# One-hots of a routing step on GpSimd instead of VectorE, and the keys of two heads in alternate partitions of the value buffers

## The chip, the cores and the metric

One core of one Trainium2 chip runs the whole kernel. The metric is the device time of an execution in microseconds; of the kernel before there are three runs with a median of 599.23 us. The engines are called TensorE (PE), VectorE (DVE), ScalarE (ACT), GpSimd (POOL) and SyncE (SP), the short names being those of the profile. SP issues most of the transfers.

## The reference

Windowed attention, and behind it a two-level mixture of experts on its output. Cut to what matters:

```python
batch, n_heads, seq, head_dim = (8, 8, 576, 64)
mask_plain = (rel >= 0) & (rel < 32)                      # heads 0 to 3
mask_dil = (rel >= 0) & (rel < 128) & (rel % 4 == 0)      # heads 4 to 7
scores = np.where(masks, scale * (q @ k.T), -1e9)
attn = exp(scores - max) ; attn = attn / (sum + 1e-09)
x = (attn @ v).transpose(0, 2, 1, 3).reshape(4608, 512)

g_logits = x @ w_group            # 4 groups: g_idx = argmax, g_w = its softmax
e_logits = x[g] @ w_expert[g]     # 4 experts a group: e_idx, e_w
for each of the 16 experts:
    h = np.maximum(xg[mask_e] @ w1[g, e], 0.0)            # 512 -> 1024
    ye = h @ w2[g, e]                                     # 1024 -> 512
    out[tok_idx] = (g_w * e_w)[:, None] * ye
```

## The kernel before

Attention runs in 36 steps n = 0 to 35, each for 64 positions of two batches and all heads, twelve groups of three steps. The loop over s from 0 to 38 works on several steps at once: `scores(s)`, `av(s - 2)`, `transpose_p(s - 1)`, `softexp(s)`, `transpose_x(s - 3)` and `normalise(s - 2)`. For one step TensorE makes the masked scores (L250, L267); VectorE takes the maximum mx (L277) and subtracts it into d (L279); ScalarE exponentiates d; TensorE transposes that (L292) into pt; then 32 matmuls (L304, `av`) multiply it with the values and with a column of ones for the sum; VectorE turns the sum into den (L353, L355) and writes the normalised x (L360). TensorE transposes x (L381) for the routing, and SP stores x to a buffer xd in device memory, three steps at a time.

The values of a group lie in `vt`, three buffers of 128 partitions, [2, 3, 8, 65] values in each: the first index is the head's half r, the second one j the step within the group. Keys of half r stand in partitions 64r to 64r + 63, in plane r; the other plane of these partitions is zero, so that one matmul over all 128 partitions serves both halves. A second copy `vs`, shifted by half a block, is made by GpSimd (`shift_v`, L128 to L138). The zeros are written at the start by ScalarE (vt[0]) and by VectorE's memsets (L916), one or two at the end of each of the first steps. Keys (`load_k`, buffers kb) already lie in alternate partitions; the third buffers of the queries and of the values are part of `wa`, which later holds weights.

Routing is done in four routes, one for each pair of batches (1152 tokens, TPB = 9 tiles of 128). `route(bp)` is a generator: matmuls of x with the router's weights, the arg-max as one-hots, the rank of each token among those of its expert by matmuls with a triangle (rk_ps), and so a slot number for each token (slots). The slot is cut into a high and a low part (sli, hl). Two sets of one-hots follow: `mv`, 9 x 64 wide, which is the token's number where the high part fits, and `ohl`, 9 x 128 wide, which is 1 where the low part fits. Nine matmuls (tb_ps, L498) add their products up into the table that says which token stands in which slot. The gains (s5, es, sg, gt) and the table's update follow.

The order of TensorE, VectorE, ScalarE and SP is that in which the code is written; only GpSimd's is set by a scheduler. A route's pieces are put between the attention's instructions by `slot()`: it stands twice in `scores`, twice in `normalise` and once in the loop, and each call runs the route up to its next `yield 0`. A `yield 2` sets `gate`, and the route goes on only after TensorE's queue has passed the next `av`. `pick(r)` chooses the two experts that start early (`early`), while attention still runs: their rows are gathered (xe), transposed (L672) and cast (xs, L673, L674). Weights come in by SP, ScalarE makes the upper half of their precision (L615) and VectorE the lower half (L612). After the last step the fourth route runs among the first matmuls of the early experts (L697).

```python
def slot():
    for _ in range(0 if gate else fine[0]):
        if run(routes) == 2:
            gate.append(1)
            break
```

Of the kernel before, what the change touches and what calls it, by code (L numbers as in the profile page):

```python
# [8 lines left out]
F32 = mybir.dt.float32  # L9
# [8 lines left out]
P = 128  # L18
# [5 lines left out]
NE = 16  # L24
# [31 lines left out]
def moe_attention_kernel(ctx, tc, q, k, k0, v, cmask, wgate, wpack, out):  # L56
# [47 lines left out]
    off = lambda t, r: t[64 * r : 64 * r + 64, 1 - r].rearrange("p j s c -> p (j s c)")  # L104
# [16 lines left out]
    def load_v(g, cuts=(0, 3)):  # L121
        for j0, j1 in zip(cuts, cuts[1:]):
            for r in range(2):
                at = slice(64 * r, 64 * r + 64)
                nc.sync.dma_start(vt[three(g)][at, r, j0:j1], v[g, at, j0:j1])

    def shift_v(g, j0=0, j1=3):
        to, own, last = vs[g % 2], vt[three(g)], vt[three(g - 1)]  # L128
        for r in range(2):
            odd, even = slice(64 * r, 64 * r + 32), slice(64 * r + 32, 64 * r + 64)  # L130
            nc.gpsimd.tensor_scalar(to[even, r, j0:j1], own[even, r, j0:j1], 1.0, 1.0, ALU.mult, ALU.mult)
            for j in range(j0, j1):
                if j > 0:
                    nc.gpsimd.tensor_scalar(to[odd, r, j], own[odd, r, j - 1], 1.0, 1.0, ALU.mult, ALU.mult)
                elif g % 3 == 0:
                    nc.gpsimd.memset(to[odd, r, 0], 0.0)
                else:
                    nc.gpsimd.tensor_scalar(to[odd, r, 0], last[odd, r, 2], 1.0, 1.0, ALU.mult, ALU.mult)  # L138
# [8 lines left out]
    for t in kb:  # L147
        nc.vector.memset(t[:, 0], 0.0)
        nc.scalar.activation(t[:, 1], id32[:, 0:1].broadcast_to([P, KW]), AF.Copy, scale=0.0)
    for r in range(2):  # L150
        z = id32[64 * r : 64 * r + 64, 0:1].broadcast_to([64, VW // 2])
        nc.scalar.activation(off(vt[0], r), z, AF.Copy, scale=0.0)
    zeros = [off(t, r) for t in (vs[0], vt[1], vs[1], vt[2]) for r in range(2)]
# [7 lines left out]
    load_q(1)  # L161
    load_v(1)
    load_q(2)
# [39 lines left out]
    mine1 = cp.tile([P, TPB], F16, name="mine1")  # L203
# [42 lines left out]
    def scores(n):  # L246
# [28 lines left out]
        d = ap.tile([P, 8, 64], F32, name="d", bufs=2)  # L275
# [3 lines left out]
        nc.vector.tensor_tensor(d, s, mx.unsqueeze(2).broadcast_to([P, 8, 64]), ALU.subtract)  # L279
# [8 lines left out]
    def transpose_p(n):  # L288
        p = st.pop(n)
        t = psT.tile([P, 4, P], F32, name="t", tag="t")  # L290
        for c in range(4):
            nc.tensor.transpose(t[:, c, :], p[:, 2 * c : 2 * c + 2, :].rearrange("p a b -> p (a b)"), id32)  # L292
# [100 lines left out]
    def route(bp):  # L393
# [52 lines left out]
        for t in range(TPB):  # L446
# [29 lines left out]
        nc.vector.tensor_tensor(  # L476
            mv,
            high.rearrange("p e k -> p (e k)").unsqueeze(1).broadcast_to([P, TPB, NE * NK4]),
            hl[:, 1].unsqueeze(2).broadcast_to([P, TPB, NE * NK4]),
            ALU.is_equal,  # L480
        )
        yield 0
        nc.vector.tensor_tensor(mv, mv, mine1.unsqueeze(2).broadcast_to([P, TPB, NE * NK4]), ALU.mult)
        yield 0
        ohl = T("ohl", [TPB, P], F16)
        for t0 in range(0, TPB, 3):
            nc.vector.tensor_tensor(
                ohl[:, t0 : t0 + 3],
                low16.unsqueeze(1).broadcast_to([P, 3, P]),
                hl[:, 0, t0 : t0 + 3].unsqueeze(2).broadcast_to([P, 3, P]),  # L490
                ALU.is_equal,
            )
            if t0 < TPB - 3:
                yield 0
# [8 lines left out]
        yield 0  # L503
# [6 lines left out]
        yield 0  # L510
# [10 lines left out]
        yield 0  # L521
# [9 lines left out]
    def pick(r):  # L531
# [3 lines left out]
        yield 0  # L535
# [12 lines left out]
        yield 0  # L548
# [344 lines left out]
    for s in range(NT + 3):  # L893
# [60 lines left out]
    while routes:  # L954
        run(routes)
    run(eq, 100)
# [227 lines left out]
```

## Time and profile before

| what | value |
| --- | --- |
| median of 3 runs | 599.23 us (597.15 to 601.65) |
| profiled execution | 596.25 us, span 594.5 us |
| mean granted clock of TensorE | 0.981 |
| busy share of the span | PE 92%, DVE 66%, ACT 54%, POOL 34% |

The profiled execution is one of its own, 1.75 us longer than its span. Shares are means over the whole span: TensorE is busy nearly all of the last two thirds and has its gaps in the first. Of the other engines it matters when they are done, more than how much they work.

### The profile page before, as it was taken

Reading aid. Unit: us, or ns where it says so; the run is one execution under the profiler, and the core shown is the slowest. Engines: PE = TensorE matmul, PEld = TensorE weight load, DVE = VectorE, ACT = ScalarE, POOL = GpSimd, SP = SyncE. Lnnn points to the kernel's source line nnn. Section 1 sums busy time; section 2 is a strip of 40 time slices with the busy share of each in tenths; the row PEclk is TensorE's granted clock in tenths of the full one; section 3 lists DMA queues with packets and bytes.
Section 4 is the critical chain, followed back from the end, with each engine's and each line's share of the span. In section 5 each row is a group of like instructions: output and inputs, shape, how many; then the busy total and the mean of one; then the engine's idle time right before and its main releaser. Section 6 shows DMA issues by size and latency. Waiting matters only on the chain. (4 is left out here: it accounts for less than half of the span.)

```text
span 594.5 us, 16716 instructions
## 1 busy us (share of the span) xinstructions
PE 544.9 (92%) x6644; PEld 392.4 (66%) x6644; DVE 394.5 (66%) x872; ACT 319.9 (54%) x568; POOL 203.1 (34%) x248
## 2 busy tenths in 40 slices
PE   4787999888697699999999999999999999999995
PEld 3666777677475457756666665756757657777883
DVE  6874595896786852556486859767476587567750
ACT  6344454553664423646364646546676566657641
POOL 6864656552401040422124152222622502202211
PEclk9999999998989799999999999999999999999999
DMA  8998988889757433495969779697897998998750
GB/s 258 304 266 227 264 245 234 250 227 229 254 142 254 132 108 139 115 299 163 244 188 289 201 240 211 218 306 203 273 244 226 300 272 237 294 298 258 246 152 29
DMA packets 83011, 134.33 MB, mean 226 GB/s; under 512 B 43532, under 2 KB 53174, under 8 KB 82930
## 3 DMA queue, kind: packets, MB, share of 16 engines
q1 hardware_dynamic: 76002, 113.65, 67.3%
q0 software_dynamic: 6784, 19.51, 10.3%
q8 instruction: 54, 0.88, 0.7%
q14 instruction: 27, 0.22, 0.2%
q10 hardware_dynamic: 144, 0.07, 0.0%
HBM read 106.16 MB, written 19.29 MB: 211 GB/s over the span
## 5 line engine op out<-in xcount | busy, mean ns | idle before, releaser
L705 DVE SCALAR_TENSOR_TENSOR hl<-a,hh 128x256 f16<-128x256 f32 (+13 forms) x144 | 60.9, 424 | 82.2 <-ACT hh L704 82.1
L761 POOL DMA_INDIRECT out<-yr,sent x31 | 34.0, 1096 | 216.4 <-ACT yr L760 204.8
L697 PE MATMUL a<-xs,wb1h 128*128 128x256 f16 (+7 forms) x576 | 99.7, 279 | 6.7 <-DVE xs L674 3.5
L697 PE MATMUL a<-xs,wa 128*128 128x304 f16 (+7 forms) x864 | 96.7, 272 | 1.8 <-DVE hl L705 1.8
L612 DVE SCALAR_TENSOR_TENSOR wa<-w,wa 128x1024 f16<-128x1024 f32 x64 | 77.8, 1224 | 28.4 <-ACT wa L615 28.4
L697 PEld LDWEIGHTS <-wa 128*128 128x128 f16 x864 | 79.3, 98 | 18.1 <-issue 2.1
L704 ACT ACTIVATE hh<-a 128x256 f16<-128x256 f32 (+13 forms) x144 | 55.8, 387 | 63.9 <-PE a L697 63.0
L790 PEld LDWEIGHTS <-hh 128*128 128x128 f16 x480 | 46.9, 98 | 54.6 <-issue 1.2
L615 ACT ACTIVATE wa<-w 128x1024 f16<-128x1024 f32 x64 | 67.2, 1054 | 22.7 <-DMA w<-wpack 21.6
L697 PE MATMUL a<-xs,wb1l 128*128 128x256 f16 (+7 forms) x288 | 79.4, 279 | 0.0
L790 PE MATMUL y<-wa,hh 128*128 128x512 f16 x240 | 73.9, 379 | 0.0
L697 PEld LDWEIGHTS <-wb1h 128*128 128x128 f16 x576 | 55.7, 99 | 16.3 <-issue 3.6
L304 PE MATMUL o<-vs,pt 128*32 128x130 f32 x576 | 43.1, 286 | 18.0 <-DVE x L360 14.6
L293 ACT COPY pt<-t 128x512 f32<-128x512 f32 x36 | 21.1, 586 | 67.9 <-PE t L292 67.9
L640 POOL DMA_INDIRECT xr<-xd,sent x41 | 41.9, 1022 | 39.9 <-DVE key L569 16.4
L612 DVE SCALAR_TENSOR_TENSOR wb2l<-w,wb2h 128x1024 f16<-128x1024 f32 x32 | 38.9, 1223 | 22.7 <-ACT wb2h L615 22.6
L304 PEld LDWEIGHTS o<-vs,pt 128*32 128x32 f32 x576 | 34.0, 114 | 23.1 <-issue 13.8
L760 ACT ACTIVATE yr<-y,cs 128x512 f32<-128x512 f32 (+3 forms) x31 | 21.3, 686 | 49.7 <-PE y L790 34.3
L790 PE MATMUL y<-wb2h,hl 128*128 128x512 f16 x120 | 45.5, 379 | 0.3 <-DVE hl L705 0.3
L790 PE MATMUL y<-wb2h,hh 128*128 128x512 f16 x120 | 45.6, 380 | 0.0
L790 PE MATMUL y<-wb2l,hh 128*128 128x512 f16 x120 | 45.5, 379 | 0.0
L790 PE MATMUL y<-wa,hl 128*128 128x512 f16 x120 | 45.5, 379 | 0.0
(199 smaller groups left out, 1072.8 us busy)
## 6 DMA issues: line engine op xcount, KB each, us to landing
w<-wpack SPq DMA_DIRECT2D x128, 512.0 KB, 5.1
kb<-k SPq DMA_DIRECT2D x24, 384.0 KB, 4.9
qb<-q SPq DMA_DIRECT2D x22, 256.0 KB, 4.1
xd<-x SPq DMA_DIRECT2D x24, 192.0 KB, 4.1
vt<-v SPq DMA_DIRECT2D x16, 260.0 KB, 5.9
vt<-v SPq DMA_DIRECT2D x16, 130.0 KB, 5.1
wa<-v SPq DMA_DIRECT2D x6, 260.0 KB, 8.9
xd<-x SPq DMA_DIRECT2D x32, 48.0 KB, 4.5
```

What stands on the lines that cost most here:

```text
L293: nc.scalar.copy(pt[n % NPT], t)
L304: nc.tensor.matmul(o[32 * j : 32 * j + 32, c // 2, at : at + 130], pt[n % NPT][:, c, 32 * j : 32 * j + 32], t[:, :, jl, bb * 4 + c, :], st ...
L612: nc.vector.scalar_tensor_tensor(l, w32, SW, h, ALU.mult, ALU.subtract)
L615: nc.scalar.mul(parts(i)[0], w32s[i], SW)
L640: nc.gpsimd.indirect_dma_start(out=xr[0:n], out_offset=None, in_=xd[0:known, :], in_offset=bass.IndirectOffsetOnAxis(ap=ent[0:n, t : t + 1 ...
L697: nc.tensor.matmul(a[:, 0:cap], ww[:, c * FF + f * P : c * FF + f * P + P], xx[:, c, 0:cap], start=(i == 0), stop=(i == len(mm) - 1),)
L704: nc.scalar.activation(hh[:, f, 0:cap], a[:, 0:cap], AF.Relu)
L705: nc.vector.scalar_tensor_tensor(hl[:, f, 0:cap], a[:, 0:cap], 0.0, hh[:, f, 0:cap], ALU.max, ALU.subtract)
L760: nc.scalar.activation(yr[0:n, :], yp[0:n, :], AF.Copy, scale=cs[0:n, t : t + 1])
L761: ins = nc.gpsimd.indirect_dma_start(out=out, out_offset=bass.IndirectOffsetOnAxis(ap=ent[0:n, t : t + 1], axis=0), in_=yr[0:n, :], in_off ...
L790: nc.tensor.matmul(yp, h[:, f, t * P : t * P + n], ww[:, f * DM : f * DM + DM], start=(i == 0), stop=(i == len(mm) - 1),)
```

## The change

Five things are changed.

1. `load_v` puts the value rows of half r into partitions r, r + 2, ..., so that the keys of both halves alternate. The exponentiated scores get the same order: d becomes [128, 4, 64, 2], written by the subtract with a stride of two, and the transposes read it without a stride. `shift_v` then works on 64 partitions and both planes at once: four instructions a group instead of eight, each with twice the columns, zeros among them.
2. The zeros: vt[0] is zeroed whole, one plane by VectorE and one by GpSimd, vt[1] by one instruction of ScalarE, vt[2] by one memset of VectorE in step 0. The copies vs need none now. The eight memsets in the first steps are gone.
3. At the start the queries of group 2 are loaded ahead of the values of group 1.
4. In routes 0 to 2 all one-hots are made by GpSimd, an `ohl` and an `mv` for each of the nine tiles, 18 instructions with per-partition operands (hl, mine1, now 32 bits) in place of VectorE's five. Route 3 has its `ohl` on GpSimd and its `mv` on VectorE as before. A `yield 2` more stands ahead of the table's matmuls in routes 0 to 2, and several `yield 0` are gone, so that two instructions run in one slot.
5. An expert whose turn has come when the routes are drained is started there.

```diff
     def load_v(g, cuts=(0, 3)):
         for j0, j1 in zip(cuts, cuts[1:]):
             for r in range(2):
-                at = slice(64 * r, 64 * r + 64)
-                nc.sync.dma_start(vt[three(g)][at, r, j0:j1], v[g, at, j0:j1])
+                nc.sync.dma_start(vt[three(g)][r:P:2, r, j0:j1], v[g, 64 * r : 64 * r + 64, j0:j1])
...
-        for r in range(2):
-            odd, even = slice(64 * r, 64 * r + 32), slice(64 * r + 32, 64 * r + 64)
-            nc.gpsimd.tensor_scalar(to[even, r, j0:j1], own[even, r, j0:j1], 1.0, 1.0, ALU.mult, ALU.mult)
+        odd, even = slice(0, 64), slice(64, P)
+        nc.gpsimd.tensor_scalar(to[even, :, j0:j1], own[even, :, j0:j1], 1.0, 1.0, ALU.mult, ALU.mult)
+        for j in range(j0, j1):
+            if j > 0:
+                nc.gpsimd.tensor_scalar(to[odd, :, j], own[odd, :, j - 1], 1.0, 1.0, ALU.mult, ALU.mult)
...
+        if i == 0:
+            nc.vector.memset(vt[0][:, 0], 0.0)
+            nc.gpsimd.memset(vt[0][:, 1], 0.0)
...
-    zeros = [off(t, r) for t in (vs[0], vt[1], vs[1], vt[2]) for r in range(2)]
+    flat = lambda t: t.rearrange("p w j s c -> p (w j s c)")
+    nc.scalar.activation(flat(vt[1]), id32[:, 0:1].broadcast_to([P, VW]), AF.Copy, scale=0.0)
...
     load_q(1)
+    load_q(2)
     load_v(1)
-    load_q(2)
...
-        nc.vector.tensor_tensor(d, s, mx.unsqueeze(2).broadcast_to([P, 8, 64]), ALU.subtract)
+        nc.vector.tensor_tensor(
+            d.rearrange("p c k w -> p c w k"),
+            s.rearrange("p (c w) k -> p c w k", w=2),
+            mx.rearrange("p (c w) -> p c w", w=2).unsqueeze(3).broadcast_to([P, 4, 2, 64]),
+            ALU.subtract,
+        )
...
-        hl = T("hl", [2, TPB], F16)
+        hl = T("hl", [2, TPB])
         nc.vector.tensor_copy(hl[:, 1], sli[:, 1])
-        yield 0
         nc.vector.scalar_tensor_tensor(hl[:, 0], hl[:, 1], -float(P), slots[:, mine], ALU.mult, ALU.add)
         yield 0
         mv = T("mv", [TPB, NE * NK4], F16)
...
         ohl = T("ohl", [TPB, P], F16)
-        for t0 in range(0, TPB, 3):
+        if bp == NBP - 1:
             nc.vector.tensor_tensor(
-                ohl[:, t0 : t0 + 3],
-                low16.unsqueeze(1).broadcast_to([P, 3, P]),
-                hl[:, 0, t0 : t0 + 3].unsqueeze(2).broadcast_to([P, 3, P]),
+                mv,
+                high.rearrange("p e k -> p (e k)").unsqueeze(1).broadcast_to([P, TPB, NE * NK4]),
+                hl[:, 1].unsqueeze(2).broadcast_to([P, TPB, NE * NK4]),
                 ALU.is_equal,
             )
-            if t0 < TPB - 3:
-                yield 0
+            nc.vector.tensor_tensor(mv, mv, mine1.unsqueeze(2).broadcast_to([P, TPB, NE * NK4]), ALU.mult)
+        for t in range(TPB):
+            nc.gpsimd.tensor_scalar(ohl[:, t], low16, hl[:, 0, t : t + 1], None, ALU.is_equal)
+            if bp < NBP - 1:
+                nc.gpsimd.tensor_scalar(
+                    mv[:, t],
+                    high.rearrange("p e k -> p (e k)"),
+                    hl[:, 1, t : t + 1],
+                    mine1[:, t : t + 1],
+                    ALU.is_equal,
+                    ALU.mult,
+                )
+        if bp < NBP - 1:
+            yield 2
         yield 2
...
-        for _ in range(2 if s == 0 else 1):
-            if zeros:
-                nc.vector.memset(zeros.pop(0), 0.0)
+        if s == 0:
+            nc.vector.memset(flat(vt[2]), 0.0)
...
+    for r in picked:
+        if r not in ev:
+            expert(r)
```

Lines of the changed kernel differ by a few from those of the kernel before (tb_ps is L502 there, x L363, d L277). VectorE's order around the one-hots of route 2, from the cast of hl on, in the kernel before (wa is a weight half, den and x belong to step 32, mx and d to step 34):

```order
L471 CAST hl<-sli 128x9
L473 SCALAR_TENSOR_TENSOR hl<-hl,slots 128x9
L279 TENSOR_TENSOR d<-s,mx 128x512
L476 TENSOR_TENSOR mv<-high,hl 128x576
L483 TENSOR_TENSOR mv<-mv,mine_209 128x576
L353 TENSOR_SCALAR den<-o 128x8
L487 TENSOR_TENSOR ohl<-low_177,hl 128x384 x2
L355 RECIPROCAL den<-den 128x8
L487 TENSOR_TENSOR ohl<-low_177,hl 128x384
L360 TENSOR_TENSOR x<-o,den 128x512
L612 SCALAR_TENSOR_TENSOR wa<-w_2558,wa 128x1024
```

and in the changed one:

```order
L473 CAST hl<-sli 128x9
L474 SCALAR_TENSOR_TENSOR hl<-hl,slots 128x9
L611 SCALAR_TENSOR_TENSOR wa<-w_2521,wa 128x1024
L275 TENSOR_REDUCE mx<-s 128x8
L277 TENSOR_TENSOR d<-s,mx 128x4x2x64
L356 TENSOR_SCALAR den<-o 128x8
L358 RECIPROCAL den<-den 128x8
L363 TENSOR_TENSOR x<-o,den 128x512
L611 SCALAR_TENSOR_TENSOR wa<-w_2523,wa 128x1024
L275 TENSOR_REDUCE mx<-s 128x8
```

The five one-hot instructions are gone from between d and x, and the weight half stands behind hl, ahead of mx.

GpSimd's order around the one-hots of route 0 in the changed kernel (vs from vt are value shifts of group 6, vs from wa those of group 5; in the kernel before the rows of shifts follow each other there):

```order
L128 TENSOR_SCALAR vs_109<-wa 64x2x520
L131 TENSOR_SCALAR vs_109<-wa 64x2x520
L128 TENSOR_SCALAR vs_108<-vt_106 64x2x1040
L131 TENSOR_SCALAR vs_108<-vt_106 64x2x520
L487 TENSOR_SCALAR ohl<-low_178,hl 128x128
L489 TENSOR_SCALAR mv<-high,hl,mine_210 128x64
```

Sixteen more of ohl and mv in turn follow; behind these come the shifts of the last third of the group:

```order
L489 TENSOR_SCALAR mv<-high,hl,mine_210 128x64
L131 TENSOR_SCALAR vs_108<-vt_106 64x2x520
L128 TENSOR_SCALAR vs_108<-vt_106 64x2x520
L135 TENSOR_SCALAR vs_109<-vt_106 64x2x520
L128 TENSOR_SCALAR vs_109<-vt_107 64x2x1040
```

TensorE's order at the end of a step of route 2 in the kernel before (t and tx are transposes, L304 is the attention's second matmul):

```order
L304 MATMUL o<-vs_109,pt_113 32x130
L304 MATMUL o<-vt_106,pt_113 32x130
L292 MATMUL t<-id_76,d 128x128 x4
L381 MATMUL tx<-id_76,x 128x128 x4
L498 LDWEIGHTS ohl
L498 MATMUL tb_ps<-mv,ohl 128x64
```

and at the same step in the changed one:

```order
L307 MATMUL o<-vs_109,pt_113 32x130
L307 MATMUL o<-vt_106,pt_113 32x130
L295 MATMUL t<-id_76,d 128x128 x4
L384 MATMUL tx<-id_76,x 128x128 x4
L671 MATMUL pt<-id_76,xe_220 128x128 x4
L307 MATMUL o<-vs_109,pt_112 32x130
```

The nine matmuls of the table have moved behind the next step's transposes; those of routes 0 and 1 stand where they stood.

## Rows read from the trace of the kernel before

**Rows 1.** The profile page, part 2: TensorE's busy tenths in 40 slices
```profile
PE   4787999888697699999999999999999999999995
```

**Rows 2.** Waits of TensorE, 0 to 226 us: us in total, times, longest
```profile
PE o L304 <- DVE x L360: 14.6, 11, 3.9
PE s L267 <- DMA kb<-k: 6.7, 3, 3.7
...
PE a L697 <- DVE xs L674: 3.5, 1, 3.5
```

**Rows 3.** Timeline, 158 to 170 us: start, us, engine, line, operation
```profile
158.72 0.16 DVE L471 CAST hl<-sli 128x9 f16<-128x9 int32 x1
...
159.59 0.75 DVE L476 TENSOR_TENSOR mv<-high,hl 128x576 f16<-128x576 f16 x1
...
160.38 0.76 DVE L483 TENSOR_TENSOR mv<-mv,mine 128x576 f16<-128x576 f16 x1
...
161.13 1.01 DVE L487 TENSOR_TENSOR ohl<-low,hl 128x384 f16<-128x384 f16 x2
...
162.60 0.68 DVE L360 TENSOR_TENSOR x<-o,den 128x512 f32<-128x512 f32 x1
...
163.43 0.61 PE L304 MATMUL o<-vs,pt 128*32 128x130 f32 x2 [3.93 <-DVE x L360]
...
168.81 0.43 PE L304 MATMUL o<-vs,pt 128*32 128x130 f32 x1
```

**Rows 4.** Windows: length, busy us by engine (count), granted clock, DMA share, GB/s
```profile
28.00:36.00 8.00, 6.06 (x126) 4.71 (x126) 6.05 (x11) 2.94 (x8) 7.22 (x11) 1.00 0.99 289
160.00:162.00 2.00, 0.00 (x0) 0.00 (x0) 1.97 (x5) 2.00 (x5) 0.00 (x0) 1.00 0.82 246
164.00:166.00 2.00, 2.00 (x33) 1.61 (x26) 1.97 (x5) 0.00 (x0) 0.00 (x0) 0.50 0.66 149
```

**Rows 5.** Timeline of SP's queue, 48 to 58 us
```profile
53.55 0.52 SPq L113 DMA_DIRECT2D kb<-k  x1
```

**Rows 6.** Groups of VectorE by form: busy us, mean ns, idle before
```profile
L916 DVE MEMSET vs<- 64x1560 f32 x4 | 5.4, 1358 | 1.3 <-issue 1.3
```

**Rows 7.** Waits of TensorE, 16 to 54 us
```profile
PE o L304 <- DVE x L360: 2.9, 3, 1.5
```

**Rows 8.** Waits of TensorE, 80 to 90 us
```profile
PE o L304 <- DVE x L360: 0.8, 1, 0.8
PE o L304 <- DVE hl L473: 0.4, 1, 0.4
```

**Rows 9.** Waits of TensorE, 116 to 126 us
```profile
PE o L304 <- DVE x L360: 1.7, 2, 1.1
```

**Rows 10.** Groups of GpSimd (POOL) by form
```profile
L134 POOL TENSOR_SCALAR vs<-vt 32x520 f32<-32x520 f32 x36 | 23.0, 641 | 4.3 <-PE o L304 1.9
L131 POOL TENSOR_SCALAR vs<-vt 32x1040 f32<-32x1040 f32 x18 | 19.0, 1054 | 12.2 <-DMA vt<-v 10.4 <-PE o L304 0.8
...
masks.py:199 POOL TENSOR_SCALAR_AFFINE_SELECT id<-id 128x128 f32<-128x128 f32 x1 | 0.3, 291 | 0.1
```

**Rows 11.** Timeline, 79 to 88 us
```profile
79.67 0.92 DVE L471 CAST hl<-sli 128x9 f16<-128x9 int32 x1
...
80.64 1.21 POOL L134 TENSOR_SCALAR vs<-vt 32x520 f32<-32x520 f32 x2
...
87.58 0.43 PE L498 MATMUL tb_ps<-mv,ohl 128*128 128x64 f16 x9
```

**Rows 12.** Groups of ScalarE by form
```profile
L388 ACT COPY xT<-tx 128x256 f32<-128x256 f32 x24 | 15.5, 647 | 0.0
...
L383 ACT COPY xT<-tx 128x256 f32<-128x256 f32 x36 | 13.2, 366 | 8.0 <-PE lt_ps L406 6.7 <-PE tx L381 1.2
```

**Rows 13.** The profile page, part 6: DMA issues, KB each, us to landing
```profile
kb<-k SPq DMA_DIRECT2D x24, 384.0 KB, 4.9
...
vt<-v SPq DMA_DIRECT2D x16, 260.0 KB, 5.9
```

More of the change, by code (lines that the diff above doesn't have):

```diff
@@ L123, in load_v @@
             for r in range(2):
-                at = slice(64 * r, 64 * r + 64)
-                nc.sync.dma_start(vt[three(g)][at, r, j0:j1], v[g, at, j0:j1])
+                nc.sync.dma_start(vt[three(g)][r:P:2, r, j0:j1], v[g, 64 * r : 64 * r + 64, j0:j1])
     def shift_v(g, j0=0, j1=3):
         to, own, last = vs[g % 2], vt[three(g)], vt[three(g - 1)]
-        for r in range(2):
-            odd, even = slice(64 * r, 64 * r + 32), slice(64 * r + 32, 64 * r + 64)
-            nc.gpsimd.tensor_scalar(to[even, r, j0:j1], own[even, r, j0:j1], 1.0, 1.0, ALU.mult, ALU.mult)
[L132 to L138, printed above, removed]
+        odd, even = slice(0, 64), slice(64, P)
[3 more added lines that the diff above has]
+                nc.gpsimd.tensor_scalar(to[odd, :, j], own[odd, :, j - 1], 1.0, 1.0, ALU.mult, ALU.mult)
+            elif g % 3 == 0:
+                nc.gpsimd.memset(to[odd, :, 0], 0.0)
+            else:
+                nc.gpsimd.tensor_scalar(to[odd, :, 0], last[odd, :, 2], 1.0, 1.0, ALU.mult, ALU.mult)
     first = ExitStack()
@@ L146, in moe_attention_kernel @@
     nc.gpsimd.memset(k0t[:, 1, 0 : 8 * 96], 0.0)
-    for t in kb:
+    for i, t in enumerate(kb):
         nc.vector.memset(t[:, 0], 0.0)
         nc.scalar.activation(t[:, 1], id32[:, 0:1].broadcast_to([P, KW]), AF.Copy, scale=0.0)
-    for r in range(2):
-        z = id32[64 * r : 64 * r + 64, 0:1].broadcast_to([64, VW // 2])
-        nc.scalar.activation(off(vt[0], r), z, AF.Copy, scale=0.0)
-    zeros = [off(t, r) for t in (vs[0], vt[1], vs[1], vt[2]) for r in range(2)]
+        if i == 0:
[3 more added lines that the diff above has]
+    nc.scalar.activation(flat(vt[1]), id32[:, 0:1].broadcast_to([P, VW]), AF.Copy, scale=0.0)
     for w in range(2):
@@ L202, in moe_attention_kernel @@
     )
-    mine1 = cp.tile([P, TPB], F16, name="mine1")
+    mine1 = cp.tile([P, TPB], F32, name="mine1")
     nc.gpsimd.iota(
@@ L274, in scores @@
         s = s.rearrange("p c w k -> p (c w) k")
-        d = ap.tile([P, 8, 64], F32, name="d", bufs=2)
+        d = ap.tile([P, 4, 64, 2], F32, name="d", bufs=2)
         mx = ap.tile([P, 8], F32, name="mx")
@@ L291, in transpose_p @@
         for c in range(4):
-            nc.tensor.transpose(t[:, c, :], p[:, 2 * c : 2 * c + 2, :].rearrange("p a b -> p (a b)"), id32)
+            nc.tensor.transpose(t[:, c, :], p[:, c].rearrange("p k w -> p (k w)"), id32)
         nc.scalar.copy(pt[n % NPT], t)
@@ L502, in route @@
         nc.vector.tensor_scalar_add(s5, s5, 1e-9)
-        yield 0
         es = T("es", [TPB, 4])
@@ L509, in route @@
         nc.vector.tensor_reduce(sg, es, axis=AX.X, op=ALU.add)
-        yield 0
         nc.vector.tensor_tensor(sg, sg, s5v[:, :, 0], ALU.mult)
@@ L534, in pick @@
         nc.vector.tensor_tensor(cnt, base[AFTER[r]], base[0], ALU.subtract)
-        yield 0
         key = T("key", [NE])
@@ L547, in pick @@
         nc.vector.tensor_tensor(kk, top[:, r], iota[:, 0:NE], ALU.mult)
-        yield 0
         nc.vector.tensor_reduce(km, kk, axis=AX.X, op=ALU.add)
```

12 lines of the change are left out of this document (removed).

## The prediction

> **What bounds the kernel now.** I read the page first, then the waits of TensorE, then the stretches where it waits. From the fifteenth slice, about 208 us, to the end the slices of TensorE show nines [rows 1]: there the experts run, nothing waits, and what the front gains or loses passes to the end one for one. All of the change lies in front of that. There TensorE's largest wait is on VectorE: 14.6 us in 11 waits stand between the attention's second matmul (L304) and the normalised output x (L360); the keys' transfers (kb) cost 6.7 us in three waits, and the first experts' input xs 3.5 us in one [rows 2]. TensorE's queue is in program order, so such a wait delays all behind it. A step needs only some 2.1 us of VectorE for mx, d and x (x 0.68 [rows 3], the others alike), less than TensorE's part of it, so VectorE is late only where something is put between: zeroing at the start, one-hots in each of four routes.
>
> Two other limits must be kept in view. In 28 to 36 us the DMA share is 0.99 [rows 4]. And SP's own issue row shows a transfer of keys sent only at 53.55 [rows 5], after a burst of x stores; TensorE then waits for it, the 3.7 us of [rows 2].
>
> **The change part by part.** The sum is made against the profiled execution, 596.25 us; the median of the runs shown, 599.23, is 3.0 us above it, which I add at the end.
>
> **Zeroing at the start.** Eight 64x1560 memsets of 1.36 us each, of which [rows 6] group four, leave steps 0 to 7. One of 3120 columns (by the same rate 2.7 us) comes to step 0, and one of 1.36 us stands ahead of that, both while TensorE still waits for its first loads. Its waits on x between 16 and 54 us are 2.9 us in three [rows 7], so 2.9 is the most that can be won; the least is nothing, because the transfers run full to 36 us [rows 4] and the next wait on keys can grow by what was won. I take 2.0: the stores that stand on SP ahead of that late transfer also come earlier when x does.
>
> **One-hots of routes 0 and 1.** VectorE loses five instructions a route: two for mv (0.75 and 0.76) and three for ohl at about 0.50 [rows 3]. The waits of TensorE that they make are 0.8 and 0.4 us in route 0 [rows 8] and 1.7 in route 1 [rows 9], 2.9 in all. GpSimd takes 18 instructions instead. Its price p for one is not in the trace, so I bound it. A 128x128 select took 0.29 us; a copy of 520 columns took 0.64 and one of 1040 columns 1.05 [rows 10], a line with a foot of 0.23 and 0.0008 per column, so 0.33 for 128 columns and 0.28 for 64. The lower end is 0.25, the upper the 520-column price, 0.64. I take 0.27 on average, as the select has the very shape, and the half-width mv is cheaper still: 18 x 0.27 = 4.9 us a route. Is that covered? In route 0 the value shifts end at 80.64 + 1.21 = 81.85 [rows 11], with hl ready by then, so the one-hots end near 86.8. TensorE reached the table's matmuls (tb_ps) at 87.58 [rows 11] after 1.2 us of waits that now are gone: 86.4. It would wait 0.4 us, in general 18p - 4.5. In route 1 the same working (there GpSimd is free a little sooner) leaves 18p - 6.0. The value shifts become fewer and longer (64 partitions with two heads' columns; by the line 6.2 us a group for 7.0), and VectorE is slowed beside them: a 9-column cast took 0.92 us beside a shift [rows 11] against 0.16 with GpSimd idle [rows 3]. I charge 0.5 us for that. Net: 2.9 - 0.4 - 0.5 = 2.0 won.
>
> No row shows an instruction of GpSimd with a per-partition operand. [...]
>
> **Route 2.** This is the largest term. Ahead of the x that ends at 163.28 VectorE runs mv at 159.59 and 160.38 and ohl from 161.13 on, three in two pieces [rows 3]. TensorE waits 3.93 us for that x, until 163.43 [rows 3], and its granted clock is then 0.50 in 164 to 166, the lower of its two levels, after 1.00 in the idle 160 to 162 [rows 4]. Without these 3.0 us x can start when its den is there, near 159.8, and end at 160.5: the wait falls to about 1.1. Waits up to 1.5 us [rows 7] cost no clock in their stretch, so I expect no fall. Before, the next L304 block came at 168.81 [rows 3], with the one at 163.43 run at half the clock. Now the block is over before 162, and the next is set by VectorE: weight cast, mx, d, x (1.2 + 3 x 0.68 from 160.5, with den between) and the transposes bring it to about 164.6. That is 4.2 us earlier, less up to 0.7 if the route's normaliser instructions (s5, es, sg) fall into the next step's path, plus as much if they are hidden. The order shows the table's nine matmuls one step later, behind the next step's transposes; GpSimd has from 159.6 to about 166.9, so 18p - 7.3 is the wait there, none at my price. I take 4.0; 2.4 if the clock falls all the same, 4.8 at best.
>
> **Route 3.** Only the three ohl (3 x 0.50) leave VectorE, ahead of the casts for xs that TensorE waits on for 3.5 us [rows 2]; GpSimd's nine take 9 x 0.29 = 2.6 us beside that wait. I take 1.4, with 0 to 1.5 as ends.
>
> **At no cost, and what covers them.** The subtract that now writes d with a stride of two: bounded by ScalarE's copies of 256 columns, 0.37 us and 0.65 us by the place they write [rows 12], so nothing or 0.3 to 0.6 us more a step; outside the routes VectorE's slack covers it, which idles for a quarter of 28 to 36 us with memsets still in it [rows 4]. Two instructions to a slot, and the gain copy with its DMA a few places earlier on ScalarE and SP: the same instructions, their places in queues that wait there for other things. The value loads into alternate partitions: 260 KB land in 5.9 us now where 384 KB of keys, already laid so, land in 4.9 [rows 13]; at nothing here, a rival below.
>
> Sum: 2.0 + 2.0 + 4.0 + 1.4 = 9.4, less 0.8 that I let the keys' wait at step 21 swallow, which stands behind route 0's gain: 8.6. So 596.25 - 8.6 = 587.6 for a profiled run, and **591** for the median.
>
> **The rivals.**
>
> *GpSimd is dear (slower).* TensorE, in order, then waits at tb_ps of each route with all that is behind it: 18p - 4.5, 18p - 6.0 and 18p - 7.3, together 54p - 17.8. Against gains of 9.8 (the 9.4 without the 0.4) it decides from p = 0.51. At 0.64 the waits are 16.8 us and the median is 599.2 + 7.0 = 606. For it: two scalars are read from memory in each mv, and the one-hots stand ahead of the value shifts of the group's last third, for which L304 waits. Against: a select and a copy of this width come to 0.29 to 0.33. 0.13.
>
> *GpSimd is dearer, but not so dear.* If each per-partition operand adds half of the foot of 0.23, ohl costs 0.40 and mv 0.48, and 18 of them 7.9 us: waits of 3.4, 1.9 and 0.6, 5.5 more than I counted; the median is 596.5. 0.15. [...]
>
> *The transfers take the gain.* SP and the transfers are nearly full to 60 us and again later; what TensorE wins at the start and in routes 0 and 1 comes back as longer waits on keys at steps 12 and 21. Then only routes 2 and 3 and half a microsecond remain: 599.2 - 5.9 = 593.3. For it: such a wait of 3.7 us is there already. Against: it ends on a transfer that SP issues late, behind stores which also move. 0.20.
>
> *The value loads get faster.* At the keys' rate 260 KB take 3.3 us for 5.9 [rows 13]; the full stretch to 36 us shortens, and the keys' wait at step 12 shrinks by some 3.5 us: 587.5. For it: that the keys of the same bytes per partition do go faster. Against: they are sent alone, and the share there is of all 16 engines. 0.15. [...]
>
> *The strided write is dear,* 0.6 us on each of 36 subtracts, of which some ten stand in steps without slack: 591 + 6 with the routes' gain halved, about 601. 0.04.
>
> **How the numbers follow.** My forecast, 587 to 595 by the ends of its own terms, has 0.33, the rivals the chances above. The range takes in fast loads together with all of route 2's gain (584) and goes up into dear GpSimd (602). A measurement of this kernel can tell about 1%, 593.2 to 605.2. Faster holds three quarters of the forecast, most of the fast loads, half of the transfers' case and a fifth of the dearer GpSimd: 0.52. Slower holds most of the first rival: 0.10. The same is the rest, 0.38.
>
> **What would show it.** In the changed profile: ohl and mv on GpSimd at 0.25 to 0.33 on average; no wait over 0.5 us before tb_ps; x of step 32 some 3 us earlier beside the step's start, with no lower clock behind it; no memset in steps 1 to 7; d still near 0.69; keys' waits at steps 12 and 21 about as now. I am wrong if tb_ps waits on GpSimd, if L304's waits on value shifts grow, or if the keys' waits grow by what the waits on x lose.

## The result

The changed kernel takes 603.07 us (median of 20 runs, 600.91 to 607.95) where the kernel before takes 599.65 beside it (20 runs). The ratio is 1.0078, with a 95% interval of 1.0058 to 1.0098: 0.8% slower, where I had forecast 1.4% faster, and the time lies above the 602 at which my range ended. The ratio goes by the fast runs alone, so it isn't quite that of the two medians (1.0057). The profiled execution has a span of 600.5 us against 594.5; the profiled run of the changed kernel, 602.38 us, lies near its median, that of the kernel before, 596.25, at the low end of its 20 (from 596.26), so the 6.0 us between the two profiles are more than the 0.8%.

**What the profile shows after.** The waits of TensorE from the start to 232 us answer to [rows 2] (engine, line, what it waited for: us in total, times, longest):

```profile
PE o L307 <- DVE x L363: 12.7, 9, 2.1
PE tb_ps L502 <- POOL mv L489: 9.5, 11, 1.0
PE s L265 <- DMA kb<-k: 7.2, 3, 3.3
...
PE o L307 <- DVE km L543: 2.4, 1, 2.4
```

Ahead of the table's matmuls a new wait of 9.5 us stands, in eleven pieces of 0.5 to 1.0 us: TensorE is done with one tile and waits for GpSimd's next pair. The wait on x looks shorter, 12.7 us for 14.6, but it isn't. The fourth line is a wait on x too (timeline of route 1):

```profile
136.26 0.96 DVE L535 TENSOR_TENSOR cnt<-base,base 128x16 f32<-128x16 f32 x1
137.26 0.99 DVE L537 SCALAR_TENSOR_TENSOR key<-cnt,low 128x16 f32<-128x16 f32 x1
138.18 0.68 DVE L363 TENSOR_TENSOR x<-o,den 128x512 f32<-128x512 f32 x1
138.78 0.15 DVE L543 TENSOR_REDUCE km<-key 128x1 f32<-128x16 f32 x1
...
139.00 0.38 PE L307 MATMUL o<-vs,pt 128*32 128x130 f32 x2 [2.38 <-DVE km L543]
```

There is one buffer for o, so the first of a step's o matmuls waits for the x before it, and in this trace it starts 0.14 to 0.15 us behind an x each time it waits. The short km, 0.15 us, only ended last. With this line, one of 1.1 us (cse) and one of 0.9 (sli) the changed kernel waits 17.1 us on x, the kernel before, counted in the same way, 16.4; 12.7 of those come after step 13 begins. The x at 138.18 stands behind VectorE's tab, cnt and key, which take 0.84 to 0.99 us here and 0.17 to 0.22 in the kernel before: value shifts, late behind the one-hots, run beside them (from 134.15 to 138.23).

GpSimd's groups by form (busy us, mean ns; idle before) answer to [rows 10]:

```profile
L487 POOL TENSOR_SCALAR ohl<-low,hl 128x128 f16<-128x128 f16 x36 | 25.2, 705 | 12.5 <-DVE hl L474 9.8 <-DVE den L358 2.7
...
L128 POOL TENSOR_SCALAR vs<-vt 64x2080 f32<-64x2080 f32 x9 | 17.3, 1925 | 12.0 <-DMA vt<-v 11.5
L489 POOL TENSOR_SCALAR mv<-high,hl,mine 128x64 f16<-128x64 f16 x27 | 17.2, 639 | 4.7 <-DVE hl L473 4.7
```

An ohl costs 0.705 us on the mean and an mv of half its width 0.639; I had counted 0.27. The longest value shifts are 1.9 us each. (A group's shift is made in two calls, so it is five instructions here and ten in the kernel before, by 60 and 120 in the traces, not the four and eight of the section on the change.) The timeline of route 0 shows one-hots and matmuls together:

```profile
76.91 0.61 POOL L487 TENSOR_SCALAR ohl<-low,hl 128x128 f16<-128x128 f16 x1 [1.30 <-DVE den L358]
77.53 0.58 POOL L489 TENSOR_SCALAR mv<-high,hl,mine 128x64 f16<-128x64 f16 x1
...
83.87 0.19 PE L502 MATMUL tb_ps<-mv,ohl 128*128 128x64 f16 x1 [0.54 <-POOL mv L489]
```

From 76.91 to 87.23 GpSimd makes the 18 one-hots, 0.59 us for an ohl and 0.57 for an mv, while VectorE works on d, mx and x beside it. Of all 63 one-hots 56 take no longer than 0.61. The other seven take 0.97 to 1.90 and raise the mean; each of them overlaps a weight half (L611) or an mv of route 3 on VectorE. One of them (timeline):

```profile
175.05 1.43 DVE L611 SCALAR_TENSOR_TENSOR wa<-w,wa 128x1024 f16<-128x1024 f32 x1
...
175.63 1.30 POOL L489 TENSOR_SCALAR mv<-high,hl,mine 128x64 f16<-128x64 f16 x1
```

In route 0 TensorE comes to tb_ps at 83.0, takes the five tiles that are ready, and then waits 3.4 us in four pieces. Behind that its clock is 0.50, the lower of the two levels in the trace (windows as in [rows 4], the clock third from the end):

```profile
88.00:92.00 4.00, 4.00 (x67) 3.37 (x65) 2.10 (x7) 0.83 (x2) 3.76 (x4) 0.50 0.79 224
168.00:176.00 8.00, 6.03 (x123) 5.06 (x123) 6.93 (x14) 6.23 (x13) 8.00 (x14) 1.00 0.71 177
176.00:184.00 8.00, 4.31 (x80) 3.53 (x75) 6.23 (x25) 4.35 (x12) 3.21 (x5) 1.00 0.48 129
```

In route 2, the other two lines, it stays at 1.00, as forecast: the wait on x there fell from 3.93 us to 0.9. But 2.8 us of waits on GpSimd came in its place, and 1.1 on the next step's x (the line on cse, a small instruction that ended last). TensorE's waits from 162 to 182 us:

```profile
PE tb_ps L502 <- POOL mv L489: 2.8, 3, 1.0
PE o L307 <- DVE cse L633: 1.1, 1, 1.1
...
PE o L307 <- DVE x L363: 0.9, 1, 0.9
```

Where each kernel stands is seen from the time at which its step n begins (the mask's matmul in TensorE's timeline, us from the start of the span):

| step | 12 | 13 | 18 | 20 | 24 | 25 | 30 | 35 | span |
| --- | --- | --- | --- | --- | --- | --- | --- | --- | --- |
| before | 53.1 | 64.4 | 83.4 | 91.0 | 109.6 | 113.4 | 132.3 | 158.1 | 594.5 |
| after | 47.8 | 58.7 | 79.9 | 92.9 | 110.3 | 115.9 | 141.8 | 167.8 | 600.5 |
| after - before | -5.3 | -5.7 | -3.5 | +1.9 | +0.7 | +2.5 | +9.5 | +9.7 | +6.0 |

Up to step 13 the changed kernel gains 5.7 us, much more than I had counted. Steps 13 to 17 lose 2.2, the steps of route 0's table (18 and 19) 5.4; steps 20 to 23 give 1.2 back, as the keys' wait at step 21 is gone; step 24 loses 1.8, and steps 25 to 29, with route 1's table and the x behind it, 7.0. From step 35 on, with routes 2 and 3, 3.7 come back in this pair of profiles.

**Two more rows.** In step 15 VectorE's subtract of 180 columns, 0.34 us in all four routes of the kernel before, takes as long as the value shift beside it (timeline):

```profile
67.09 2.00 POOL L128 TENSOR_SCALAR vs<-wa 64x2080 f32<-64x2080 f32 x1
...
67.23 2.06 DVE L444 TENSOR_TENSOR df<-lg,mx 128x180 f32<-128x180 f32 x1
```

And the transfers move more in the stretch that was full. Window 12 to 36 us, first of the kernel before, then of the changed one (last two columns: DMA share, GB/s):

```profile
12.00:36.00 24.00, 19.66 (x394) 14.88 (x389) 20.13 (x31) 9.14 (x20) 20.61 (x30) 1.00 1.02 296
```

```profile
12.00:36.00 24.00, 24.00 (x518) 19.68 (x514) 16.19 (x34) 12.47 (x28) 20.34 (x17) 1.00 0.95 335
```

TensorE is busy all of that window now. A value load lands in 4.6 us instead of 5.9 (the page's DMA issues, as [rows 13]):

```profile
kb<-k SPq DMA_DIRECT2D x24, 384.0 KB, 4.3
...
vt<-v SPq DMA_DIRECT2D x16, 260.0 KB, 4.6
```

### The profile page after: what moved, and what is told of

It is laid out like the page before. It is cut to its first block, busy times and chain, and to the rows that moved or that the text cites. A ratio compares the mean times of both kernels' runs of the same rounds, so it can differ in the third digit from the quotient of the medians.

```text
span 600.5 us, 16688 instructions
## 1 busy us (share of the span) xinstructions
PE 545.0 (91%) x6644; PEld 394.1 (66%) x6644; DVE 387.7 (65%) x848; ACT 320.8 (53%) x567; POOL 234.6 (39%) x252
## 5 line engine op out<-in xcount | busy, mean ns | idle before, releaser
L611 DVE SCALAR_TENSOR_TENSOR wa<-w,wa 128x1024 f16<-128x1024 f32 x64 | 78.3, 1233 | 24.1 <-ACT wa L614 24.1
L307 PE MATMUL o<-vs,pt 128*32 128x130 f32 x576 | 42.1, 285 | 17.1 <-DVE x L363 12.7
L611 DVE SCALAR_TENSOR_TENSOR wb2l<-w,wb2h 128x1024 f16<-128x1024 f32 x32 | 38.9, 1223 | 23.9 <-ACT wb2h L614 23.9
L275 DVE TENSOR_REDUCE mx<-s 128x8 f32<-128x512 f32 x36 | 24.7, 685 | 38.2 <-PE s L265 38.2
```

Source lines behind the costliest of these rows:

```text
L275: nc.vector.tensor_reduce(mx, s, axis=AX.X, op=ALU.max)
L307: nc.tensor.matmul(o[32 * j : 32 * j + 32, c // 2, at : at + 130], pt[n % NPT][:, c, 32 * j : 32 * j + 32], t[:, :, jl, bb * 4 + c, :], st ...
L611: nc.vector.scalar_tensor_tensor(l, w32, SW, h, ALU.mult, ALU.subtract)
```

## The experiments

The theory after the first comparison (A): GpSimd's one-hots are dear by themselves, TensorE waits for the last of them and loses clock, and the layout part alone is a gain. The rival (B): the layout with its longer shifts is what costs. The level of the kernel before lay between 599.7 and 604.8 us from one set of runs to another, so ratios to its own runs beside each kernel are compared, and one profile of each for the steps.

**Each half alone.** The first kernel has the value layout, zeroing and load order as changed and the routes as before; the second the routes (and the early experts' start) as changed and the rest as before.

```diff
 # the first, against the changed kernel
-        for t in range(TPB):
-            nc.gpsimd.tensor_scalar(ohl[:, t], low16, hl[:, 0, t : t + 1], None, ALU.is_equal)
+        for t0 in range(0, TPB, 3):
+            nc.vector.tensor_tensor(
+                ohl[:, t0 : t0 + 3],
...
 # the second, against the changed kernel
-                nc.sync.dma_start(vt[three(g)][r:P:2, r, j0:j1], v[g, 64 * r : 64 * r + 64, j0:j1])
+                nc.sync.dma_start(vt[three(g)][at, r, j0:j1], v[g, at, j0:j1])
...
```

> The changed kernel with the routes as before: all one-hots on VectorE with their slots; value layout, shifts, zeroing and load order as changed. Theory A (a one-hot instruction costs GpSimd about 0.58 us by itself, TensorE waits for the last ones at tb_ps and loses clock; the layout part alone is a gain): the 5.3 us won up to step 12 stay, the waits before tb_ps are gone, some 3.4 us of the start's gain are lost in steps 15 and 24 where small VectorE instructions stand behind long value shifts: 595 to 598 us. Theory B (the layout with its longer shifts is what costs, the one-hots on GpSimd pay): 603 or more.

> The kernel before with only the routes changed (one-hots on GpSimd, fewer slots, the one yield more). Theory A: route 0 costs about 5.4 us by steps 18 and 19, route 1 about 6.9 by steps 27 to 30, route 2 gives back 3.7: 606 to 610 us, with ohl and mv near 0.6 us each. Theory B: 594 to 598 us, since the routes' gain then stands alone.

Measured: 0.9941 (0.9905 to 0.9977), 596.92 us, for the layout alone, and 1.0138 (1.0077 to 1.0200), 608.73, for the one-hots alone. Both are where theory A had them, and B falls. The two effects differ by 2%; the change as a whole is their product (0.994 x 1.014 = 1.008). The second kernel's one-hots have the same prices, 0.707 and 0.638 us on the mean, and TensorE waits for them as in the changed kernel (start to 230 us):

```profile
PE tb_ps L499 <- POOL mv L486: 10.4, 11, 1.0
```

Its profiled run is the longest of its four, 612.11 us, and step 13 begins at 71.4 us in it for 64.4, though up to there it does the same as the kernel before but for the type of mine1: single profiles can differ that much in the start. From step 13 to step 30 it takes 10.9 us more than the kernel before, and from there to the end 2.0 less.

**The price of a GpSimd instruction.** Behind the last route, where nothing reads the results, forms of the instruction were run, first two of each, then six of nine forms in turn.

```diff
+            for _ in range(6):
+                nc.gpsimd.tensor_scalar(du, low16, a, None, ALU.is_equal)
+                nc.gpsimd.tensor_scalar(du, low16, 1.0, None, ALU.is_equal)
+                nc.gpsimd.tensor_scalar(du, low16, a, None, ALU.mult)
+                nc.gpsimd.tensor_scalar(du, low16, 1.0, None, ALU.mult)
...
```

> The changed kernel with 18 more GpSimd instructions behind the last route, two of each form, whose results nobody reads, for their durations alone. If the per-partition operand is what makes a one-hot dear: 0.58 with one for 128 columns of 16 bits, about 0.30 with a number in its place, in 16 and in 32 bits alike. If the 16-bit type is: 0.58 with and without, about 0.30 in 32 bits. If it is a fixed price of any such instruction: all six short forms 0.5 to 0.6, and 1152 columns with one operand about 1.5, far under nine times 0.6.

> The changed kernel with 54 more GpSimd instructions behind the last route, six of each of nine forms in turn, whose results nobody reads. VectorE works beside them, so the least of each six is read. If the compare is dear: multiply 0.30 with a number and near that with an operand, compare 0.5 to 0.6 both ways. If the operand is dear: compare and multiply alike, 0.3 without and 0.55 with it. If both add up: 0.30, 0.35 to 0.45 with an operand, 0.5 for the compare, 0.6 for both.

Measured in the second, one round of the timeline: L533 and L534 compare 128 columns with an operand and with a number, L535 and L536 multiply likewise; L539 and L540 compare and multiply 64 columns with two operands and with two numbers; L541 multiplies 64 columns twice with two operands.

```profile
226.34 0.61 POOL L533 TENSOR_SCALAR ohl<-low,hl 128x128 f16<-128x128 f16 x1
227.03 0.53 POOL L534 TENSOR_SCALAR ohl<-low 128x128 f16<-128x128 f16 x1
227.66 0.60 POOL L535 TENSOR_SCALAR ohl<-low,hl 128x128 f16<-128x128 f16 x1
228.34 0.53 POOL L536 TENSOR_SCALAR ohl<-low 128x128 f16<-128x128 f16 x1
228.98 0.58 POOL L539 TENSOR_SCALAR ohl<-high,hl,mine 128x64 f16<-128x64 f16 x1
229.65 0.43 POOL L540 TENSOR_SCALAR ohl<-high 128x64 f16<-128x64 f16 x1
230.18 0.39 POOL L541 TENSOR_SCALAR ohl<-high,hl,mine 128x64 f16<-128x64 f16 x1
```

And of the first, the groups of two multiplies by the number 1.0, in 16 and in 32 bits, which is the form of the value shifts:

```profile
L538 POOL TENSOR_SCALAR ohl<-low 128x128 f16<-128x128 f16 x2 | 0.6, 299 | 0.2
L542 POOL TENSOR_SCALAR rks<-low 128x128 f32<-128x128 f32 x2 | 0.6, 298 | 0.2
```

So it is not the 16-bit type (in 32 bits the compare takes the same, 0.60 with an operand and 0.53 with a number), and the operand is the smaller part: a single operation with a number costs 0.53, compare and multiply alike, an operand adds 0.07 and two add 0.15. In a pair the compare does count: with two operands and 64 columns compare and multiply take 0.58, two multiplies 0.39. Only pairs of multiplies are cheap, 0.30 for 128 columns with numbers. None of the expectations has this. What is dear is the rate more than the start of an instruction. Nine times the columns with one compare and one operand, also in the first run, where about 1.5 us had been expected if the price were a fixed one (group of two; the lesser took 3.25):

```profile
L555 POOL TENSOR_SCALAR ohl<-low,hl 128x1152 f16<-128x1152 f16 x2 | 6.7, 3354 | 0.2
```

From 0.61 for 128 columns and 3.25 for 1152 a column comes to 0.0026 us, an estimate from two widths, against the 0.0008 of the pairs of multiplies in [rows 10]. The rows from which I had drawn the price, shifts and a select, were of the cheap kinds.

**Shorter shifts.** With the one-hots on VectorE, each value shift is cut by head half and step, to 520 columns on 64 partitions, twelve instructions a group for five.

```diff
-        nc.gpsimd.tensor_scalar(to[even, :, j0:j1], own[even, :, j0:j1], 1.0, 1.0, ALU.mult, ALU.mult)
+        for w in range(2):
+            for j in range(j0, j1):
+                nc.gpsimd.tensor_scalar(to[even, w, j], own[even, w, j], 1.0, 1.0, ALU.mult, ALU.mult)
...
```

> As the first of these kernels (one-hots on VectorE), but each value shift cut by head half and step to 520 columns on 64 partitions, twelve instructions a group instead of four. If VectorE's small instructions wait for the GpSimd instruction that runs, to its end: the 2 us of one such instruction in steps 15 and 24 fall to about 0.7, and the kernel is 2 to 4 us faster than the first. If the time that GpSimd reads altogether counts: no faster, and a little slower for twelve times the fixed part.

> The short shifts' kernel again, for its interval and beside the three others: a ratio to the kernel before of 0.985 to 0.990, 7 to 9 us less.

Measured: 0.9858 (0.9771 to 0.9945), and again 0.9858 (0.9810 to 0.9906). It beats both kernels, by 1.4% the one before. VectorE's subtract in step 15, first with long shifts (one-hots on VectorE), then in the two profiles with short ones (timelines):

```profile
67.62 2.06 DVE L444 TENSOR_TENSOR df<-lg,mx 128x180 f32<-128x180 f32 x1
```

```profile
70.01 0.34 DVE L445 TENSOR_TENSOR df<-lg,mx 128x180 f32<-128x180 f32 x1
```

```profile
68.76 0.77 DVE L445 TENSOR_TENSOR df<-lg,mx 128x180 f32<-128x180 f32 x1
```

In the second df took 0.34 us, as in the kernel before, and in the third 0.77: over the four routes df takes up to 2.06 us with long shifts and at most 0.77 with short ones. So the length of the one GpSimd instruction that df meets counts, not the sum, as GpSimd spends 93.0 and 94.4 us on the short shifts for 74.6 on the long ones. Not every VectorE instruction is held: in the changed kernel a d of 0.69 us ran at 134.20, beside a shift from 134.15 to 136.08. Which are held no run here settles: df and d read two tiles each, the cast that took 0.92 us beside a shift [rows 11] reads one.

The same cut in the changed kernel as a whole:

> The changed kernel whole, with each value shift cut to 520 columns. If the long shifts cost what the first batch shows (about 5 us, by small VectorE instructions held behind them) and this adds to the cost of the one-hots: 597 to 600 us for the 603 of the changed kernel. If the shifts' cost shows only where VectorE makes the one-hots: 602 to 604.

Measured: 1.0069 (1.0033 to 1.0105), no gain beside 1.0078, as the second expectation had it. TensorE's waits from the start to 230 us, with the shifts cut:

```profile
PE tb_ps L503 <- POOL mv L490: 12.3, 13, 1.0
PE o L308 <- DVE x L364: 9.6, 9, 2.5
```

The long wait of route 1 is gone, and the waits on x fall from 17.1 us to 11.7 in all; those at tb_ps grow by 2.8 and those for keys by 0.9. With the one-hots on it GpSimd is what TensorE waits for, and the twelve shifts take longer than the five. The ratio shows no gain; by the intervals one of up to some 3 us could hide in it.

**The table a step later.** The changed kernel with one more gate ahead of tb_ps in routes 0 and 1:

```diff
-        if bp < NBP - 1:
-            yield 2
-        yield 2
+        for _ in range((3, 3, 2, 1)[bp]):
+            yield 2
```

> The changed kernel whole, with one yield 2 more ahead of the table's matmuls in routes 0 and 1, so that TensorE comes to them a step later; GpSimd's one-hots cost what they cost. If TensorE's waits at tb_ps and the clock behind them are the cost: 3.4 us of waits and 2.4 of clock in route 0, about as much in route 1, go: 593 to 597 us at the level of the first comparison, a ratio of 0.989 to 0.996 for 1.008. If GpSimd is full there and what stands behind the one-hots (the value shifts, the choice of an expert) is late in their place: 1.002 to 1.010.

Measured: 0.9988 (0.9950 to 1.0026), between the two expectations. TensorE's waits from the start to 230 us:

```profile
PE o L307 <- DVE x L363: 14.4, 9, 4.0
...
PE tb_ps L501 <- POOL mv L489: 4.5, 5, 1.0
PE o L307 <- DVE km L542: 3.6, 1, 3.6
```

Five microseconds of waits at tb_ps are gone, and the clock stays at 1.00 from 82 to 132 us, behind the tables of both routes (step 20 begins at 86.8 for 92.9, step 30 at 130.0 for 141.8). What follows from the table is late instead, and meets the next value shifts: ahead of the x behind the km line tab takes 1.94 us, cnt 0.97 and key 0.99, and ahead of the x for which it waits 4.0 us two instructions of route 2 take 1.56 and 1.10 (0.33 alone). The waits on x come to 19.6 us for 17.1. Steps 30 to 34 take 32.4 us for 26.0, with a clock of 0.79 in 132 to 140 and 0.77 in 150 to 162.

**GpSimd for a part of routes 2 and 3.** The kernel with short shifts, with only the ohl of these two routes on GpSimd:

```diff
+        if bp >= NBP - 2:
+            for t in range(TPB):
+                nc.gpsimd.tensor_scalar(ohl[:, t], low16, hl[:, 0, t : t + 1], None, ALU.is_equal)
+            if bp == NBP - 2:
+                yield 2
```

> The short shifts' kernel with only the ohl of routes 2 and 3 on GpSimd (nine instructions each, one yield more in route 2), all else of the one-hots on VectorE. Theory A (a GpSimd one-hot costs some 0.6 us, so it pays only where nothing else fills GpSimd and TensorE comes late to tb_ps): nine take 5.5 to 8 us and are over before tb_ps of route 2; its wait on x falls from 2.9 by about 1.3, route 3's xs wait by 1.4: 588 to 590 us for the 592 of the short shifts. If the waits only move to something else that is late there: 591 to 593.

Measured: 0.9861 (0.9808 to 0.9914), the same as without, as the second expectation had it. Nine instructions run from 156.75 to 163.64, so they are in time; TensorE doesn't wait at tb_ps of route 2. The wait on x there fell from 2.9 us (3.9 in the second profile of the kernel without) to 2.1, as VectorE's two mv, 0.75 and 0.81 us, still stand ahead of that x. Nothing is won by this.

**What made the start faster.** Four kernels: zeroing alone taken off VectorE in the kernel before; in the kernel with short shifts, the load order back, the memsets back, and the value rows back in 64 neighbouring partitions (which makes the attention's output another one).

```diff
 # memsets back, first on memory beside the third buffers, then on a free table
+        for _ in range(5 if 1 <= s < 7 else 0):
+            nc.vector.memset(perm, 0.0)
...
 # value rows in one block
-                nc.sync.dma_start(vt[three(g)][r:P:2, r, j0:j1], v[g, 64 * r : 64 * r + 64, j0:j1])
+                nc.sync.dma_start(vt[three(g)][at, r, j0:j1], v[g, at, j0:j1])
```

> The kernel before with only the zeroing moved: the four memsets of the copies vs by GpSimd, those of vt[1] by ScalarE, those of vt[2] by VectorE in step 0; keys and values laid out and loaded as before. If the zeroing made the start's gain of 5.3 us: step 12 begins near 49 for 53 us, and the median is 595 to 597. If the loads into alternate partitions made it: step 12 begins where it did or a little earlier, 598 to 600.

> The short shifts' kernel (one-hots on VectorE) with the values of group 1 loaded ahead of the queries of group 2 again, as before the change. If the order made the start's gain: TensorE waits on queries at step 3 and step 12 begins at 52 us or later, 2 us or more above the short shifts' kernel. If not: step 12 begins at 47 to 50 us and the time is the same within 1.5 us.

> The short shifts' kernel with VectorE's memsets of 1.36 us each put back into steps 1 to 6, on memory that nobody reads. If VectorE's zeroing cost the start 2.9 us as my prediction's term has it: step 12 begins 2 to 3 us later, 51 to 53 us, and the kernel is 2 to 3 us slower. If the transfers alone set the start: it begins where it did.

> The short shifts' kernel (one-hots on VectorE) with 1.3 to 1.4 us of VectorE memsets in each of steps 1 to 6 again, five of 256 columns on a table that is written much later, so that none waits for a transfer. If VectorE's zeroing cost the start time once the loads are fast: TensorE waits on x 2 to 3 us in steps 4 to 8 and step 12 begins at 50 to 52 us for 48 to 49.6; ratio to the kernel before 0.989 to 0.991. If the transfers set the start alone: step 12 as before this edit and a ratio of 0.984 to 0.988.

> The short shifts' kernel with the value rows of each head half loaded into 64 neighbouring partitions, as before the change, while all else takes them to alternate: the attention's output is then another one, so only the stretch up to step 12 is read. If the partitions of the loads made the start's gain: a value load takes 5.5 to 6 us for 4.1 to 4.6, and step 12 begins at 52 us or later. If not: 4 to 4.6 us and 47 to 50.

| kernel | ratio to before | step 12 begins | step 13 begins |
| --- | --- | --- | --- |
| short shifts, two profiles | 0.9858 | 49.6, 48.1 | 61.5, 60.2 |
| load order back | 0.9857 (0.9796 to 0.9919) | 50.1 | 62.3 |
| memsets back, free | 0.9883 (0.9845 to 0.9922) | 53.8 | 61.8 |
| value rows in one block | not read | 56.5 | 69.1 |
| zeroing alone, in the kernel before | 1.0047 (1.0007 to 1.0087) | 54.9 | 66.5 |

The load order does nothing that these runs can tell. Zeroing alone, moved to GpSimd and ScalarE, doesn't help either: the waits on x go, and waits on transfers take their place. The first run with memsets back, 0.9993, tells nothing, since one memset waited 7.7 us for a transfer into the same buffer; the second shows the mechanism (its five memsets take 1.84 us a step together, a third more than the 1.36 meant). TensorE's waits from 16 to 62 us, first with the memsets, then without (the second run of short shifts):

```profile
PE o L308 <- DVE x L364: 5.6, 4, 2.5
PE s L266 <- DMA kb<-k: 1.8, 1, 1.8
```

```profile
PE s L266 <- DMA kb<-k: 5.4, 2, 4.4
...
```

VectorE's zeroing costs 5.6 us of waits, and the keys' waits give 3.6 back; step 13 begins 0.3 and 1.6 us later than in the two profiles without, and the ratio, 0.9883 for 0.9858, is not clear of them. So the term is real on VectorE and mostly taken by the transfers. The value loads are what counts. With one block, 12 to 36 us (last two columns: DMA share, GB/s):

```profile
12.00:36.00 24.00, 18.50 (x322) 14.28 (x323) 11.12 (x23) 7.11 (x14) 17.71 (x30) 0.93 1.03 284
```

and with alternate partitions, the same kernel otherwise (the second run of short shifts):

```profile
12.00:36.00 24.00, 23.56 (x511) 18.64 (x506) 16.37 (x34) 12.05 (x27) 21.38 (x36) 1.00 0.95 334
```

The nearly full engines move 284 or 334 GB/s by where the rows go, and step 13 begins at 69.1 or at 60.2. One profile of a start is no sure measure, but all of them together say the same: with blocks step 13 begins at 64.4, 66.5, 69.1 and 71.4 us, with alternate partitions at 58.1 to 62.3 in eleven profiles (69.0 in the run with the memset that waited).

## Why the prediction was wrong

**The step that failed is the price of an instruction in "One-hots of routes 0 and 1": "I take 0.27 on average, as the select has the very shape".** An ohl costs 0.59 us and an mv 0.57, and 0.705 and 0.639 on the mean. The waits that the working hung on it are of the right kind, and too large rather than too small. With p = 0.58 its 18p - 4.5, 18p - 6.0 and 18p - 7.3 give 5.9, 4.4 and 3.1 us; measured are 3.4, 3.4 and 2.8. In route 0 this is because GpSimd was free sooner than I had read: the one-hots begin 6.1 us ahead of TensorE (76.91 and 83.02), not 4.5. What the working left out came on top: the clock's fall in steps 19 and 28 (5.57 and 4.37 us for 3.14), 2.4 and 1.2 us.

The first rival, with its decision at p = 0.51, is what happened, and I had given it 0.13. At p = 0.58 its own formula gives 602.9 us. That this is so near the 603.07 is in part luck: the start is 3.7 us better than counted and the waits are 4.0 smaller than the formula's 13.5, while the clock and the long shifts cost some 9 more than it has for them. The bounds were not too narrow, as 0.64 was the upper one; the choice between them was wrong, since the row nearest in shape is not the one nearest in form.

**The clock:** "Waits up to 1.5 us [rows 7] cost no clock in their stretch" is right for that stretch, where the clock is 1.00 from 16 to 54 us, but it was no ground for the tables. Four waits of 0.54 to 0.95 us in a row were followed by 0.50 in route 0; three of 0.86 to 0.95 in route 2 left it at 1.00. What decides between the two stays open.

**The value shifts:** "I charge 0.5 us" for VectorE beside longer shifts was some eight times too low. Steps 13 to 17 lose 2.2 us to the kernel before and step 24 1.8; with the one-hots on VectorE and the same long shifts they lose 2.2 and 1.7, with short shifts 0.0 to 0.4 each. The wait of 2.4 us in route 1, behind tab, cnt and key, comes on top. So the waits on x, which the change was to cut by taking work off VectorE, stay as long as they were (17.1 us for 16.4); with short shifts they are 11.7. By the ratios with long and short shifts (0.9941 and 0.9858, one-hots on VectorE) the length costs 0.8% or 5.0 us, some 3 us either way by the intervals. I had the row that shows it, the cast of 0.92 us, and I reckoned with sums of GpSimd time where the length of a single instruction decides. In the changed kernel as a whole cutting the shifts showed no gain: the waits on x fall by 5.4 us, and those at tb_ps grow by 2.8.

**Zeroing at the start:** the term said 2.0, "2.9 is the most that can be won", and the gain by step 13 is 5.7. The bound was too low, as it took the waits on x alone. From 16 to 62 us TensorE waits 9.5 us in the kernel before, 3.7 of it for keys, 2.9 for x, 1.1 for queries and 1.8 in small pieces. In the changed one all of that is gone but the keys' wait, which hardly grew:

```profile
PE s L265 <- DMA kb<-k: 3.9, 2, 3.0
```

By the experiments the zeroing alone would have been swallowed by waits on transfers, as the rival on these had it. The gain is that of the other rival, the value loads, which had 3.5 us in the text and a chance of 0.15. (Its reason, keys of the same bytes per partition, is misread: 384 KB on 64 partitions are more than 260 KB on as many.) I weighed the two rivals apart, though both say that the transfers set the start.

**Route 2** went as its text says, in mechanism: the wait fell from 3.93 to 0.9 (1.1 forecast), and the clock stayed up. With route 3 it gave 3.7 us for the 5.4 counted, as tb_ps waits there too. **Route 3's** wait on xs fell from 3.5 to 2.0, near the 1.4 forecast. **The strided write** costs nothing: d takes 0.691 us for 0.688.

## What to carry to other kernels

Take the price of an instruction on GpSimd from a row of its own form, with the same count of operations and operands; where there is none, a chain that waits for 18 of them is a risk to be weighed at the upper bound. Work handed to a second engine is free only if that engine's whole list, started when its inputs are there, ends before the reader arrives; if it doesn't, an engine in program order pays for it with all that is queued behind. Where small VectorE instructions stand beside GpSimd's, keep GpSimd's instructions short, unless another engine waits for GpSimd already; and where transfers are full, ask first where their rows land.

## What the runs showed that I had not expected

- GpSimd's two multiplies by a number take 0.30 us for 128 columns; one multiply or one compare with a number 0.53; an operand per partition adds 0.07 us. With a compare a column costs about 0.0026 us, with two multiplies 0.0008, estimates from two widths each.
- A VectorE subtract of 0.34 us took 2.06 us beside a GpSimd shift of 2.00. Cutting the shifts to 520 columns was worth some 5 us of 597, though GpSimd then runs twelve a group for five and spends 93 us on them for 75.
- It goes the other way too: a GpSimd one-hot of 0.57 us took 1.30 beside a VectorE weight half of 1.43.
- Value rows in alternate partitions rather than in blocks of 64 moved 334 GB/s for 284 at a DMA share near 1 (0.95 and 1.03).
- A wait that the profile puts down to a VectorE instruction of 0.15 us was the wait for the x that had ended 0.14 us before TensorE's start: the instruction named was only the last to end. Read with it what ended just before.
